# 64-bit weights turned to float32 by a scaled copy of their high words, with low halves on VectorE and a new order of work

## The chip, the cores and the metric

The kernel runs on one core of a Trainium2 chip. A core has TensorE (PE in the rows, PEld its weight loads), VectorE (DVE), ScalarE (ACT), GpSimd (POOL) and SyncE (SP, which here only issues DMAs). The metric is the time of one execution on the device in microseconds, as the median of several runs.

## The reference

Three stages follow each other: a retention layer, a dense layer with `h - tanh(h)`, and an expert layer whose routing is a greedy assignment over all logits.

```python
batch, n_heads, seq, head_dim = (8, 8, 576, 64)
def _attn_ref(q, k, v):
    scores = scale * np.matmul(q, k.transpose(0, 1, 3, 2))
    Dmat = np.where(rel >= 0, gamma[:, None, None] ** rel[None, :, :], 0.0)
    return np.matmul(scores * Dmat[None, :, :, :], v).astype(np.float32)

n_tokens, d_model, d_ff = (4608, 512, 2048)
'w_in': np.random.randn(d_model, d_ff).astype(np.float32) * (1.0 / np.sqrt(d_model))
'w_out': np.random.randn(d_ff, d_model).astype(np.float32) * (1.0 / np.sqrt(d_ff))
def _moe_ref(x, w_in, w_out):
    h = x @ w_in
    g = h - np.tanh(h)
    return (g @ w_out).astype(np.float32)

N, D, E, F = (4608, 512, 8, 1024)
def _moe2_ref(x, w_gate, w1, w2):
    logits = x @ w_gate
    order = np.argsort(-logits.flatten())   # greedy, each expert takes N // E tokens
    ...
    out[mask] = np.maximum(x[mask] @ w1[e], 0.0) @ w2[e]
```

The factor `1.0 / np.sqrt(...)` is a 64-bit scalar, so `w_in` and `w_out` arrive as 64-bit floats. They reach the chip as pairs of 32-bit words, and the kernel makes float32 values of them itself.

## The kernel before, in words

**Stages.** `phase_ab` does the retention layer and the dense layer, `phase_c` the routing and the experts. Tokens go in 12 blocks of 384 (`n`); a block needs four head pairs (`hp`) of the retention layer, so there are 48 pairs `k`. The hidden width of 2048 is cut in 16 pieces `f`. A step `s` is one layer of one block: `h_mm` multiplies the block with one piece of `w_in`, eight instructions on ACT and DVE (`act_in`, `act_do`) make `h - tanh(h)`, `g_high` and `g_low` split it, and `x2_mm` multiplies it with one piece of `w_out`. All products are made of high and low parts, so every operand is first split in two float32r tiles: the high part by a copy on ACT, the low part by a subtraction on POOL or DVE.

**Weights.** There are 32 halves `j`: 16 pieces of `w_in` and 16 of `w_out`, each 128 x 512 values of 64 bits, 512 KB. A half is loaded (`conv_load`, three buffers, `wst` in the rows), then goes through six steps in `work` (six buffers): `bits` (two DVE instructions, L207 and L208, which take the sign, the exponent and the upper bits of the mantissa from the high word), `low` (ACT, L217, the low word as a number), `square` (ACT, L212, the square of the high word), `plus` (POOL, L222, adds the low bits), `guard` (DVE, L226, sets values that would be too small to zero, by the square), `split_hi` (ACT, L231) and `split_lo` (L237: every third half on DVE, the others on POOL, by `CD = 3`). In all of them the words are read and written where they lie, high and low words in turn, so with gaps of one word.

**Pairs.** `attn_load` loads a pair by four DMAs of 192 KB (L261, tiles named after weight tiles in which they lie: `w1h`, `w1l`, `w0h`, `w0l`), `v_scale` scales its values (two ACT instructions, L272), `attn_scores` (L290) and `attn_kv` (L305) are matmuls, `mask` (L317) and `attn_state` run on DVE, `attn2` (L357, L367) on PE and `attn_out` (L387, tile `xf`) on DVE. Four pairs make a block; its values are split (`x_high`, `x_low`) before the first `h_mm`.

**What sets the order.** The first 12 pairs, the 32 halves and the first 34 steps (blocks 0 and 1 and the first two of block 2) are handed as tasks to a list scheduler (`Tasks`) when the program is built. It takes the ready task that can begin first on its engine, and among equals the one with the highest weight in the table `W`; each task has a cost in microseconds, and a task with a `lock` also holds a port that DVE and POOL share in the plan. What it picks is the order of the instructions on every engine, and each engine then works its queue strictly in that order. From step 34 on, the order is written out by hand and the change does not touch it; steps of blocks 2 to 11 load one pair after another in between. The DMAs of qkv and of the weights are all issued on SP in the planned order; four small tables (`qtab`, `vtab`, `amask`, `cint`) are loaded by DMAs on ACT at the very start.

The lines that the steps below use: L157 to L160 (tables), L200 (load of a half), L207 to L237 (its steps), L261 (load of a pair), L272 (`v_scale`), L305 (`attn_kv`), L426 (`h_mm`), L450 to L456 (`act_do`), L470 (`g_low`), L489 (`x2_mm`), L508 (store of a finished block).

Of the kernel before, what the change touches and what calls it, by code (L numbers as in the profile page):

```python
# [36 lines left out]
W = {'a2': 4, 'bits': -3, 'do0': 2, 'do1': -1, 'do2': -4, 'do3': 2, 'end': 2, 'gate': 1, 'gh': -2, 'h': -3, 'hi': -2, 'in0': 2, 'in1': 4, 'in2': -2, 'in3': -2, 'kv': 1, 'lo': -1, 'load': -2, 'low': -1, 'mask': 1, 'out': 2, 'plus': -1, 'raw': 3, 'square': 1, 'state': 2, 'v': -1, 'x2': -3, 'x2h': -4, 'xl': -1, 'xo': 1}  # L37
# [12 lines left out]
CD = 3  # L50
# [90 lines left out]
def phase_ab(tc, ctx, qkv, wio, wgt, wgk, ident, qtab, vtab, amask, cint, x2d, L):  # L141
# [47 lines left out]
    raw = [r.rearrange("p (w t) -> p w t", t=2) for r in raw]  # L189
# [23 lines left out]

    def low(j):

        lw = at(j)[1]
        nc.scalar.activation(lw, lw.bitcast(U32), AF.Copy, scale=2.0 ** -29)  # L217

    def plus(j):

        _, lw, pi, _ = at(j)
        nc.gpsimd.tensor_tensor(pi, pi, lw, op=OP.add)  # L222

    def guard(j):
        H, _, _, p = at(j)
        nc.vector.scalar_tensor_tensor(p, H.bitcast(F32), F64_TINY ** 2, p, op0=OP.is_ge, op1=OP.mult)  # L226

    def split_hi(j):
        io, f = halves[j]
        WH[io][f] = wtile("h", io, f)  # L230
        nc.scalar.activation(WH[io][f].rearrange("p k m -> p (k m)"), at(j)[3], AF.Copy)  # L231

    def split_lo(j):
        io, f = halves[j]
        WL[io][f] = wtile("l", io, f)
        hi, lo = (w[io][f].rearrange("p k m -> p (k m)") for w in (WH, WL))
        (nc.vector if j % CD == 0 else nc.gpsimd).tensor_tensor(lo, at(j)[3], hi.bitcast(F32), op=OP.subtract)  # L237

# [361 lines left out]
    def layer(s):  # L600
# [657 lines left out]
def lay_out(q, k, v, moe_w_in, moe_w_out, moe2_w_gate, moe2_w1, moe2_w2):  # L1258
# [45 lines left out]
```

## Time and profile before

| | |
|---|---|
| median of 3 runs | 1548.69 us (1546.82 to 1548.99) |
| profiled execution, its own time | 1549.22 us |
| its span (first to last instruction) | 1547.4 us |
| mean granted TensorE clock | 0.975 of full speed |
| busy: PE / DVE / ACT / POOL | 1452.7 / 1132.5 / 759.9 / 558.3 us |
| first matmul of the dense layer (L426) | at 42.83 us |
| last of the 12 planned pairs leaves DVE (L387) | at 101.30 us |
| last use of a half on DVE or POOL | at about 208 us |
| blocks 0 and 1 stored (L508) | at 227.1 and 228.97 us |
| blocks 2 and 3 stored | at 314.77 and 394.28 us |

The page gives busy times of each engine, the chain of waits that ended last, and groups of instructions. A stretch of the trace can be asked for apart: then the busy time of each engine in it, its granted clock and its DMA share are given, also for the instructions of one line alone. Since each engine works its queue in order, what matters is which engine is never idle in a stretch, and what the others wait for in it.

### The profile page before, as it was taken

The page shows a single profiled execution, that of the slowest core. Times are in us where ns is not written, and L with a number is a line of the kernel's source. Part 1 is how long each engine was busy: PE and PEld are TensorE (multiplying, and loading weights), DVE is VectorE, ACT ScalarE, POOL GpSimd, SP SyncE. Part 2 cuts the span into 40 slices and gives each one's busy share as a digit, 9 for nine tenths or more (in the row PEclk, how much of TensorE's full clock was granted, in tenths as well). Part 3 has the DMA queues.
Part 4 walks back from the last instruction along what each step waited for, and adds up shares of the span by engine and source line. Part 5 has one row for each costly group of instructions (what it writes and reads, how often), then busy time and mean ns, then how long its engine had stood idle before and what let it go on. Part 6 is the DMA issues. An engine that isn't in the chain of part 4 may idle for free.

```text
span 1547.4 us, 26175 instructions
## 1 busy us (share of the span) xinstructions
PE 1452.7 (94%) x9500; PEld 1273.1 (82%) x9500; DVE 1132.5 (73%) x2741; ACT 759.9 (49%) x1584; POOL 558.3 (36%) x492
## 2 busy tenths in 40 slices
PE   5989899999999999999999999937999999999997
PEld 4777788899898989898989898826788787887996
DVE  7999966878787878787878787867676776765210
ACT  4767775555656555656555656503332323424421
POOL 4546551212222222222222223225535526446541
PEclk7999999999999999999999999968999999999999
DMA  7622231111111111111111100014433423426220
GB/s 255 199 75 82 80 113 68 43 62 42 62 42 62 42 62 42 62 42 62 42 62 42 63 3 21 1 38 130 135 92 110 135 87 113 135 83 191 90 65 31
DMA packets 48610, 122.43 MB, mean 79 GB/s; under 512 B 6624, under 2 KB 13408, under 8 KB 48224
## 3 DMA queue, kind: packets, MB, share of 16 engines
q1 hardware_dynamic: 41184, 99.80, 19.5%
q0 software_dynamic: 6144, 19.93, 4.0%
q8 instruction: 75, 1.23, 0.3%
q10 hardware_dynamic: 1152, 1.02, 0.2%
q14 instruction: 55, 0.45, 0.1%
HBM read 101.85 MB, written 18.87 MB: 78 GB/s over the span
## 4 chain that ended last, share of the span: by engine, by line
PE 73%; DVE 15%; issue 4%; ACT 3%; POOL 2%; DMA 1%; SPq 0%; ACTq 0%; POOLq 0%; DVEq 0%
PE x L489 21%; PE h L426 21%; PE ff L1189 12%; PE ff L1158 10%; PE pb L290 2%; PE pb L357 2%; PE pb L369 1%; DVE work L208 1%; DVE t L456 1%; DVE t L450 1%; PE tp L1112 1%; PE pb L305 1%; DVE t L452 1%; DVE work L207 1%; DVE h L454 1%
## 5 line engine op out<-in xcount | busy, mean ns | idle before, releaser
L470 POOL TENSOR_TENSOR gl<-t,gh 128x384 fp32r<-128x384 f32 x192 | 200.3, 1043 | 644.3 <-ACT gh L467 560.6
L426 PE MATMUL h<-xh,w0h 128*128 128x384 f32 x704 | 239.7, 340 | 7.4 <-DVE t L456 7.3
L426 PE MATMUL h<-xh,w0l 128*128 128x384 f32 x704 | 237.4, 337 | 0.0
L436 ACT ACTIVATE S<-h 128x384 f32<-128x384 f32 x192 | 93.5, 487 | 285.6 <-PE h L426 285.5
L489 PE MATMUL x<-w1h,gh 128*128 128x512 f32 x576 | 230.7, 400 | 0.7 <-ACT gh L467 0.7
L489 PE MATMUL x<-w1l,gh 128*128 128x512 f32 x576 | 226.1, 393 | 0.0
L489 PE MATMUL x<-w1h,gl 128*128 128x512 f32 x576 | 217.1, 395 | 1.5 <-POOL gl L470 1.0
L450 DVE SCALAR_TENSOR_TENSOR t<-t,S 128x384 f32<-128x384 f32 x192 | 114.2, 595 | 119.8 <-ACT t L439 118.8
L530 DVE SCALAR_TENSOR_TENSOR junk<-x2r,wg 128x512 f32<-128x512 f32 x240 | 167.3, 697 | 5.1
L426 PE MATMUL h<-xl,w0h 128*128 128x384 f32 x704 | 152.3, 337 | 0.3 <-DVE xl L413 0.3
L426 PEld LDWEIGHTS h<-xh,w0h 128*128 128x128 f32 x704 | 132.4, 188 | 18.5 <-DVE t L456 11.6
L1075 POOL TENSOR_TENSOR w2l<-ws,w2h 128x512 fp32r<-128x512 f32 x64 | 82.5, 1292 | 161.1 <-ACT w2h L1074 158.9
L426 PEld LDWEIGHTS h<-xh,w0l 128*128 128x128 f32 x704 | 132.7, 189 | 6.9
L489 PEld LDWEIGHTS x<-w1h,gl 128*128 128x128 f32 x576 | 108.1, 188 | 29.9 <-POOL gl L470 5.8
L1189 PE MATMUL ff<-w2h,hh 128*128 128x512 f32 x320 | 127.5, 398 | 3.1 <-DVE hl L1171 2.0
L456 DVE COPY_PREDICATED t<-m,h 128x384 f32<-128x384 uint16 x192 | 114.5, 596 | 21.5 <-ACT m L445 1.7
L1189 PE MATMUL ff<-w2l,hh 128*128 128x512 f32 (+1 forms) x320 | 127.3, 398 | 0.6 <-POOL w2l L1075 0.6
L439 ACT ACTIVATE t<-S,bias 128x384 f32<-128x384 f32 x192 | 118.3, 616 | 17.6 <-POOL gl L470 1.1
L426 PEld LDWEIGHTS h<-xl,w0h 128*128 128x128 f32 x704 | 126.1, 188 | 0.9 <-DVE xl L413 0.9
L489 PEld LDWEIGHTS x<-w1h,gh 128*128 128x128 f32 x576 | 108.1, 188 | 22.8 <-ACT gh L467 1.4
L489 PEld LDWEIGHTS x<-w1l,gh 128*128 128x128 f32 x576 | 108.2, 188 | 17.0
L1158 PE MATMUL ff<-xh,w1h 128*128 128x288 f32 x512 | 115.2, 303 | 6.3 <-DVE hl L1171 5.5
(212 smaller groups left out, 2988.2 us busy)
## 6 DMA issues: line engine op xcount, KB each, us to landing
ws<-in_w SPq DMA_DIRECT2D x128, 256.0 KB, 3.1
ain<-in_qkv SPq DMA_DIRECT2D x36, 768.0 KB, 4.2
wst<-in_wio SPq DMA_DIRECT2D x32, 512.0 KB, 3.6
x2d<-x2r SPq DMA_DIRECT2D x33, 256.0 KB, 2.0
w1h<-in_qkv SPq DMA_DIRECT2D x12, 192.0 KB, 4.0
w1l<-in_qkv SPq DMA_DIRECT2D x12, 192.0 KB, 4.1
w0h<-in_qkv SPq DMA_DIRECT2D x12, 192.0 KB, 3.9
w0l<-in_qkv SPq DMA_DIRECT2D x12, 192.0 KB, 3.8
```

The lines of the kernel that those rows point to most:

```text
L290: nc.tensor.matmul(PSA[k][a][:, chunk(c)], kt[r, chunk(c)], q[r, chunk(c)], start=True, stop=True)
L426: nc.tensor.matmul(h[:, :TB], w[0][f][:, hp, :], x, start=i == 0, stop=i == 11)
L436: nc.scalar.activation(S, h, AF.Square, scale=KSC)
L439: nc.scalar.activation(AT[s][2], AT[s][1], AF.Square, bias=bias[:, 0:1])
L450: nc.vector.scalar_tensor_tensor(t, t, PA - PB * PB / 4, S, op0=OP.add, op1=OP.mult)
L456: nc.vector.copy_predicated(t, m.bitcast(U16), h)
L470: nc.gpsimd.tensor_tensor(G[s][1], TT.pop(s), G[s][0].bitcast(F32), op=OP.subtract)
L489: nc.tensor.matmul(X2[n][i], g[:, i * 128:i * 128 + 128], w, start=(f == 0 and g is gh and w is wh), stop=(f == NF - 1 and g is gl))
L530: nc.vector.scalar_tensor_tensor(j, r, 1.0, wg[e // 4][:, e % 4, :], op0=OP.mult, op1=OP.mult, accum_out=L[:, c, e:e + 1])
L1075: nc.gpsimd.tensor_tensor(l, s, h.bitcast(F32), op=OP.subtract)
L1158: nc.tensor.matmul(ps[u], w[:, k, :], x[:, k, 288 * u:288 * u + 288], start=i == 0, stop=i == 11)
L1189: nc.tensor.matmul(o, h, w, start=f == 0 and i == 0, stop=f == 7 and i == len(prods) - 1, skip_group_check=t == 4)
```

## The change

The two DVE steps `bits` and `guard` and the ACT step `square` become `shrink` (ACT) and a shorter `bits` (DVE). `shrink` reads the high word as a float32 and multiplies it by 2^-112, which moves the exponent to its place and sets too small values to zero; it writes the result without gaps into `work`. `low` now writes its words without gaps too, into the first half of the load buffer. `bits` then shifts by three into the second half of the load buffer (`tensor_scalar`, L216 of the new file) and joins the sign (`scalar_tensor_tensor`, L217), all without gaps. `plus` and `split_hi` stay, and a load buffer is free after `plus`, not after `guard`. `CD` goes from 3 to 1, so every `split_lo` (L233) is on DVE. The tables that ACT loads first change their order (`cint` first, `qtab` last). The weights `W` and the costs of tasks are new, so the list is made anew: the same tasks apart from those above come in another order.

```diff
-CD = 3
+CD = 1
...
-    nc.scalar.dma_start(out=qt, in_=qtab)
+    nc.scalar.dma_start(out=ci[:, :4], in_=cint)
     nc.scalar.dma_start(out=vt[:, :12], in_=vtab)
     nc.scalar.dma_start(out=am, in_=amask)
-    nc.scalar.dma_start(out=ci[:, :4], in_=cint)
+    nc.scalar.dma_start(out=qt, in_=qtab)
...
     def at(j):
-        return raw[j % 3][:, :, 1], raw[j % 3][:, :, 0], work[j % 6], work[j % 6].bitcast(F32)
+        r = raw[j % 3]
+        return r.rearrange("p (w t) -> p w t", t=2), r[:, :DM], r[:, DM:], work[j % 6]
+
+    def shrink(j):
+
+        words, _, _, p = at(j)
+        nc.scalar.activation(p.bitcast(F32), words[:, :, 1].bitcast(F32), AF.Copy, scale=2.0 ** -112)
+
+    def low(j):
+
+        words, lw, _, _ = at(j)
+        nc.scalar.activation(lw, words[:, :, 0].bitcast(U32), AF.Copy, scale=2.0 ** -29)
 
     def bits(j):
-        H, _, pi, _ = at(j)
-        nc.vector.tensor_scalar(pi, H, ci[:, 0:1], ci[:, 1:2], op0=OP.logical_shift_left, op1=OP.bitwise_and)
-        nc.vector.scalar_tensor_tensor(pi, H, ci[:, 2:3], pi, op0=OP.bitwise_and, op1=OP.bitwise_or)
-
-    def square(j):
-        H = at(j)[0].bitcast(F32)
-        nc.scalar.activation(H, H, AF.Square)
...
+        _, _, t, p = at(j)
+        nc.vector.tensor_scalar(t, p, ci[:, 0:1], None, op0=OP.logical_shift_left)
+        nc.vector.scalar_tensor_tensor(p, p, ci[:, 1:2], t, op0=OP.bitwise_and, op1=OP.bitwise_or)
...
-    def guard(j):
-        H, _, _, p = at(j)
-        nc.vector.scalar_tensor_tensor(p, H.bitcast(F32), F64_TINY ** 2, p, op0=OP.is_ge, op1=OP.mult)
...
-        add(("raw", j), SP, DMA_HALF, lambda: conv_load(j), get("guard", j - 3), [get("raw", j - 1)])
-        add(("bits", j), VE, 1.05, lambda: bits(j), get("raw", j), get("lo", j - 6), lock=1.05)
-        add(("low", j), AE, 0.52, lambda: low(j), get("raw", j))
-        add(("square", j), AE, 0.52, lambda: square(j), get("bits", j))
-        add(("plus", j), GE, 1.23, lambda: plus(j), get("bits", j), get("low", j), lock=1.23)
-        add(("guard", j), VE, 0.65, lambda: guard(j), get("square", j), get("plus", j), lock=0.65)
-
+        add(("raw", j), SP, DMA_HALF, lambda: conv_load(j), get("plus", j - 3), [get("raw", j - 1)])
+        add(("shrink", j), AE, 0.58, lambda: shrink(j), get("raw", j), get("lo", j - 6))
+        add(("low", j), AE, 0.58, lambda: low(j), get("shrink", j))
+        add(("bits", j), VE, 1.12, lambda: bits(j), get("low", j), lock=1.12)
+        add(("plus", j), GE, 1.31, lambda: plus(j), get("bits", j), lock=1.31)
```

How the queues stand, at the three places that the prediction speaks of. On ACT, the start of the program before, after the four table loads (`wst_100` and `wst_101` hold the first three halves, `w0h_108` and `w0h_112` the values of pairs 0 and 1):

```order
L217 ACT_TABLE_LOAD
L217 ACTIVATE wst_100<-wst_100 128x512
L212 ACTIVATE wst_100<-wst_100 128x512
L217 ACTIVATE wst_100<-wst_100 128x512
L217 ACTIVATE wst_101<-wst_101 128x512
L212 ACTIVATE wst_100<-wst_100 128x512
L231 ACTIVATE w0h_159<-work 128x512
L212 ACTIVATE wst_101<-wst_101 128x512
L272 ACTIVATE w0h_108<-w0h_108,vt 128x3x64 x2
L272 ACTIVATE w0h_112<-w0h_112,vt 128x3x64 x2
```

Seven steps of the weights stand ahead of the values of pair 0. The same place on ACT now (L268 is `v_scale`, L207 `shrink`, L212 `low`, L227 `split_hi`, L405 `x_high`):

```order
L268 ACT_TABLE_LOAD
L268 ACTIVATE w0h_108<-w0h_108,vt 128x3x64 x2
L268 ACTIVATE w0h_112<-w0h_112,vt 128x3x64 x2
L207 ACTIVATE work<-wst_100 128x512
L212 ACTIVATE wst_100<-wst_100 128x512
L207 ACTIVATE work<-wst_100 128x512
L212 ACTIVATE wst_100<-wst_100 128x512
L227 ACTIVATE w0h_231<-work 128x512
```

The values of pairs 0 and 1 now come first, then two halves. On SP, which issues the loads, the start before:

```order
L200 DMA wst_100<-in_wio 128x1024 x2
L200 DMA wst_101<-in_wio 128x1024
L261 DMA w1h_106<-in_qkv 128x384
L261 DMA w1l_107<-in_qkv 128x384
L261 DMA w0h_108<-in_qkv 128x384
L261 DMA w0l_109<-in_qkv 128x384
```

Three halves are loaded ahead of pair 0. The start on SP now:

```order
L257 DMA w1h_106<-in_qkv 128x384
L257 DMA w1l_107<-in_qkv 128x384
L257 DMA w0h_108<-in_qkv 128x384
L257 DMA w0l_109<-in_qkv 128x384
L257 DMA w1h_110<-in_qkv 128x384
L257 DMA w1l_111<-in_qkv 128x384
L257 DMA w0h_112<-in_qkv 128x384
L257 DMA w0l_113<-in_qkv 128x384
L198 DMA wst_100<-in_wio 128x1024 x2
L257 DMA w1h_114<-in_qkv 128x384
```

Pairs 0 and 1 go first, then two halves, then pair 2. On DVE, in the stretch after the last planned pair, where layers and halves alternate, before:

```order
L207 TENSOR_SCALAR work<-wst_101,ci 128x512
L208 SCALAR_TENSOR_TENSOR work<-wst_101,ci,work 128x512
L207 TENSOR_SCALAR wst_101<-wst_100,ci 128x512
L208 SCALAR_TENSOR_TENSOR wst_101<-wst_100,ci,wst_101 128x512
L450 SCALAR_TENSOR_TENSOR t<-t,S 128x384
L452 TENSOR_TENSOR t<-t,h 128x384
L454 TENSOR_TENSOR h<-T,h 128x384
L456 COPY_PREDICATED t<-m,h 128x384
L450 SCALAR_TENSOR_TENSOR t<-t,S 128x384
L226 SCALAR_TENSOR_TENSOR work<-wst_101,work 128x512
```

Two halves' `bits` stand together ahead of a layer, and a `guard` inside the next. In the same stretch now (L446 to L452 are the four steps of a layer, L233 `split_lo`, L216 and L217 `bits`):

```order
L446 SCALAR_TENSOR_TENSOR t<-t,S 128x384
L448 TENSOR_TENSOR t<-t,h 128x384
L450 TENSOR_TENSOR h<-T,h 128x384
L233 TENSOR_TENSOR w1l_1456<-work,w1h_1450 128x512
L452 COPY_PREDICATED t<-m,h 128x384
L216 TENSOR_SCALAR wst_100<-wst_101,ci 128x512
L217 SCALAR_TENSOR_TENSOR wst_101<-wst_101,ci,wst_100 128x512
L446 SCALAR_TENSOR_TENSOR t<-t,S 128x384
```

Each layer now carries one `split_lo` and one `bits`. Up to the last planned pair there are 13 halves and 7 layers on DVE, where before there were 17 `bits` and 6 layers. After it 19 halves are left, spread over 22 layers up to the last `split_lo`, where before 15 were spread over 22.

## Rows read from the trace of the kernel before

**Rows 1.** The page: busy time of each engine, and the chain by engine.

```profile
PE 1452.7 (94%) x9500; PEld 1273.1 (82%) x9500; DVE 1132.5 (73%) x2741; ACT 759.9 (49%) x1584; POOL 558.3 (36%) x492
PE 73%; DVE 15%; issue 4%; ACT 3%; POOL 2%; DMA 1%; SPq 0%; ACTq 0%; POOLq 0%; DVEq 0%
```

**Rows 2.** Stretches: start:end, length, busy us of each engine, clock, DMA, GB/s.

```profile
core 0: us, PE busy (x) PEld busy (x) DVE busy (x) ACT busy (x) POOL busy (x), PEclk, DMA share, GB/s
0.00:16.23 16.23, 5.72 (x26) 2.42 (x26) 7.17 (x11) 6.05 (x10) 5.19 (x8) 0.85 0.77 261
16.23:42.83 26.60, 20.63 (x212) 15.76 (x212) 24.10 (x48) 16.03 (x33) 14.22 (x11) 0.71 0.78 268
42.83:101.30 58.47, 50.55 (x443) 40.52 (x442) 54.49 (x104) 38.16 (x75) 30.57 (x24) 0.94 0.47 146
101.30:205.70 104.40, 96.34 (x467) 83.12 (x468) 96.94 (x140) 77.72 (x154) 61.77 (x47) 1.00 0.20 66
205.70:229.00 23.30, 22.68 (x114) 20.25 (x114) 15.37 (x28) 18.15 (x39) 9.58 (x9) 1.00 0.35 134
315.00:394.50 79.50, 79.44 (x502) 71.32 (x501) 63.90 (x156) 44.52 (x96) 18.77 (x18) 1.00 0.15 50
```

**Rows 3.** Who waited for whom, PE, 0 to 230 us: total, times, longest.

```profile
PE h L426 <- DVE t L456: 13.0, 16, 3.5
```

**Rows 4.** Timeline of PE: start, length, what, [idle before and releaser].

```profile
9.09 0.94 PE L290 MATMUL ps<-w1h,w1l 64*128 64x128 f32 x12 [3.06 <-DMA w1l<-in_qkv]
16.23 1.25 PE L305 MATMUL ps<-w0h,w0l 128*64 128x64 f32 x12 [6.20 <-ACT w0h L272]
42.83 0.45 PE L426 MATMUL h<-xh,w0h 128*128 128x384 f32 x1
```

**Rows 5.** Timeline of ACT at the start.

```profile
5.09 0.68 ACT L217 ACTIVATE wst<-wst 128x512 int32<-128x512 uint32 x1 [0.76 <-DMA wst<-in_wio]
15.17 0.67 ACT L212 ACTIVATE wst<-wst 128x512 f32<-128x512 f32 x1 [1.59 <-DVE work L208]
15.74 1.48 ACT L272 ACTIVATE w0h<-w0h,vt 128x192 f32<-128x192 f32 x4
```

**Rows 6.** Stretches for L207, L208, L226, L237 in turn: before 16.23, and 0 to 230.

```profile
0.00:16.23 16.23, 2.59 (x3) 0.85 0.77 261
sum 230.00, DVE 25.93; mean DVE 5.19
0.00:16.23 16.23, 3.17 (x3) 0.85 0.77 261
sum 230.00, DVE 36.68; mean DVE 7.34
0.00:16.23 16.23, 0.68 (x1) 0.85 0.77 261
sum 230.00, DVE 26.98; mean DVE 5.40
0.00:16.23 16.23, 0.69 (x1) 0.00 (x0) 0.85 0.77 261
sum 230.00, DVE 9.33 POOL 30.71; mean DVE 1.87 POOL 6.14
```

**Rows 7.** Lines L207 and L208: duration min/median/max in ns.

```profile
L207 DVE TENSOR_SCALAR work<-wst,ci x22: 534/544/1505, 8.8 to 196.7; 128x512 int32<-128x512 int32 x22
L208 DVE SCALAR_TENSOR_TENSOR work<-wst,ci,work x22: 751/754/1701, 9.4 to 197.5; 128x512 int32<-128x512 int32 x22
```

**Rows 8.** Timelines of POOL and DVE, one stretch held by another engine.

```profile
10.30 1.46 POOL L222 TENSOR_TENSOR work<-work,wst 128x512 int32<-128x512 int32 x1 [8.61 <-DVE work L208]
...
10.65 1.67 DVE L208 SCALAR_TENSOR_TENSOR work<-wst,ci,work 128x512 int32<-128x512 int32 x1
```

**Rows 9.** Groups by line, 0 to 230 us: count, busy us, mean ns, idle before.

```profile
L470 POOL TENSOR_TENSOR gl<-t,gh 128x384 fp32r<-128x384 f32 x33 | 37.4, 1133 | 61.3 <-ACT gh L467 41.3 <-issue 9.6 <-PE x L489 5.2
L212 ACT ACTIVATE wst<-wst 128x512 f32<-128x512 f32 x32 | 21.6, 674 | 24.6 <-DVE work L208 15.0 <-DVE wst L208 9.5
```

More of the change, by code (lines that the diff above doesn't have):

```diff
@@ L35 @@
 WARM = 14
-W = {'a2': 4, 'bits': -3, 'do0': 2, 'do1': -1, 'do2': -4, 'do3': 2, 'end': 2, 'gate': 1, 'gh': -2, 'h': -3, 'hi': -2, 'in0': 2, 'in1': 4, 'in2': -2, 'in3': -2, 'kv': 1, 'lo': -1, 'load': -2, 'low': -1, 'mask': 1, 'out': 2, 'plus': -1, 'raw': 3, 'square': 1, 'state': 2, 'v': -1, 'x2': -3, 'x2h': -4, 'xl': -1, 'xo': 1}
+W = {'a1': 3, 'a2': 0, 'bits': -4, 'do0': 0, 'do1': -3, 'do2': -4, 'do3': -2, 'end': -3, 'gate': -1, 'gh': -1, 'gl': 1, 'h': 0, 'hi': 0, 'in0': 1, 'in1': 4, 'in2': -1, 'in3': -3, 'kv': 2, 'lo': -2, 'load': 3, 'low': -2, 'mask': -2, 'out': 2, 'plus': -1, 'raw': 3, 'shrink': -2, 'state': -2, 'v': 2, 'x2': 0, 'x2h': -4, 'xh': 1, 'xl': 1, 'xo': 3}
 SLACK = 0.0
@@ L188, in phase_ab @@
     raw = [wst[0][:, :2 * DM], wst[0][:, 2 * DM:], wst[1][:, :2 * DM]]
-    raw = [r.rearrange("p (w t) -> p w t", t=2) for r in raw]
     work = [bw.tile([128, DM], I32, tag="x2r", name="work", bufs=3) for _ in range(3)]
@@ L199, in conv_load @@
         io, f = halves[j]
-        nc.sync.dma_start(out=raw[j % 3], in_=wio[f, io].bitcast(I32).rearrange("p (w t) -> p w t", t=2))
+        nc.sync.dma_start(out=raw[j % 3], in_=wio[f, io].bitcast(I32))
     def at(j):
-        return raw[j % 3][:, :, 1], raw[j % 3][:, :, 0], work[j % 6], work[j % 6].bitcast(F32)
-    def bits(j):
-        H, _, pi, _ = at(j)
-        nc.vector.tensor_scalar(pi, H, ci[:, 0:1], ci[:, 1:2], op0=OP.logical_shift_left, op1=OP.bitwise_and)
-        nc.vector.scalar_tensor_tensor(pi, H, ci[:, 2:3], pi, op0=OP.bitwise_and, op1=OP.bitwise_or)
-    def square(j):
-        H = at(j)[0].bitcast(F32)
-        nc.scalar.activation(H, H, AF.Square)
-    def low(j):
-        lw = at(j)[1]
-        nc.scalar.activation(lw, lw.bitcast(U32), AF.Copy, scale=2.0 ** -29)
-    def plus(j):
-        _, lw, pi, _ = at(j)
-        nc.gpsimd.tensor_tensor(pi, pi, lw, op=OP.add)
-    def guard(j):
-        H, _, _, p = at(j)
-        nc.vector.scalar_tensor_tensor(p, H.bitcast(F32), F64_TINY ** 2, p, op0=OP.is_ge, op1=OP.mult)
+        r = raw[j % 3]
[6 more added lines that the diff above has]
+        nc.scalar.activation(lw, words[:, :, 0].bitcast(U32), AF.Copy, scale=2.0 ** -29)
+    def bits(j):
+        _, _, t, p = at(j)
+        nc.vector.tensor_scalar(t, p, ci[:, 0:1], None, op0=OP.logical_shift_left)
+        nc.vector.scalar_tensor_tensor(p, p, ci[:, 1:2], t, op0=OP.bitwise_and, op1=OP.bitwise_or)
+    def plus(j):
+        _, lw, _, p = at(j)
+        nc.gpsimd.tensor_tensor(p, p, lw, op=OP.add)
     def split_hi(j):
@@ L230, in split_hi @@
         WH[io][f] = wtile("h", io, f)
-        nc.scalar.activation(WH[io][f].rearrange("p k m -> p (k m)"), at(j)[3], AF.Copy)
+        nc.scalar.activation(WH[io][f].rearrange("p k m -> p (k m)"), at(j)[3].bitcast(F32), AF.Copy)
     def split_lo(j):
@@ L236, in split_lo @@
         hi, lo = (w[io][f].rearrange("p k m -> p (k m)") for w in (WH, WL))
-        (nc.vector if j % CD == 0 else nc.gpsimd).tensor_tensor(lo, at(j)[3], hi.bitcast(F32), op=OP.subtract)
+        (nc.vector if j % CD == 0 else nc.gpsimd).tensor_tensor(lo, at(j)[3].bitcast(F32), hi.bitcast(F32), op=OP.subtract)
     pairs = [(n, hp) for n in range(NB) for hp in range(4)]
@@ L566, in conv_half @@
         io, f = halves[j]
-        add(("raw", j), SP, DMA_HALF, lambda: conv_load(j), get("guard", j - 3), [get("raw", j - 1)])
-        add(("bits", j), VE, 1.05, lambda: bits(j), get("raw", j), get("lo", j - 6), lock=1.05)
-        add(("low", j), AE, 0.52, lambda: low(j), get("raw", j))
-        add(("square", j), AE, 0.52, lambda: square(j), get("bits", j))
-        add(("plus", j), GE, 1.23, lambda: plus(j), get("bits", j), get("low", j), lock=1.23)
-        add(("guard", j), VE, 0.65, lambda: guard(j), get("square", j), get("plus", j), lock=0.65)
+        add(("raw", j), SP, DMA_HALF, lambda: conv_load(j), get("plus", j - 3), [get("raw", j - 1)])
[3 more added lines that the diff above has]
+        add(("plus", j), GE, 1.31, lambda: plus(j), get("bits", j), lock=1.31)
         old = {p: get("a2", 8 + late.index((io, f, p)) // 4) if (io, f, p) in late else None for p in "hl"}
-        add(("hi", j), AE, 0.52, lambda: split_hi(j), get("guard", j), old["h"])
-        us = 0.62 if j % CD == 0 else 1.23
+        add(("hi", j), AE, 0.55, lambda: split_hi(j), get("plus", j), old["h"])
+        us = 0.68 if j % CD == 0 else 1.36
         add(("lo", j), VE if j % CD == 0 else GE, us, lambda: split_lo(j), get("hi", j), old["l"], lock=us)
@@ L614, in layer @@
         add(("gh", s), AE, 0.41, lambda: g_high(s), get("do", s, 3), get("x2", s - 2))
-        add(("gl", s), GE, 0.96, lambda: g_low(s), get("gh", s), lock=0.96)
+        add(("gl", s), GE, 1.04, lambda: g_low(s), get("gh", s), lock=1.04)
         if s == NJ:
@@ L1267, in lay_out @@
     wio = np.ascontiguousarray(np.stack([wi, moe_w_out.reshape(NF, 128, DM)], axis=1)).view(np.int64)
-    cint = np.tile(np.array([3, 0x3FFFFFF8, 0xC0000000, 0xFF800000], np.uint32).view(np.int32), (128, 1))
+    cint = np.tile(np.array([3, 0x80000000, 0, 0], np.uint32).view(np.int32), (128, 1))
     g = np.array(GAM)
```

5 lines of the change are left out of this document (2 added, 3 removed).

## The prediction

> **What bounds the kernel now.** I read the page first, for the engine that fills the span; then the stretches, for where it is not filled; then who PE waits for there, and the rows of the waited-for engine line by line. Over the whole span PE is busy 94% and holds 73% of the chain, DVE 15% [rows 1]. From 315 us on, in a whole block, PE is busy 79.44 of 79.5 us: nothing done to the weights can help there, since their last half is through at about 208 us. The change acts on the first 229 us, up to the store of blocks 0 and 1. There the reader is to see two things [rows 2]. From 16.23 to 205.70 us DVE is busy 24.10 + 54.49 + 96.94 = 175.5 of 189.5 us, 93%, while PE has 167.5 us: DVE is the bound, and PE's idle time in front of the layers is put down to DVE, 13.0 us [rows 3]. Up to 16.23 us nobody is the bound: PE stands 6.20 us for the scaled values of pair 0 [rows 4], which on ACT stand behind a square that waits for DVE [rows 5].
>
> **Part 1, the start.** Before, the first `attn_kv` runs at 16.23 us [rows 4], after the scaling at 15.74 us [rows 5]. Now pair 0 is the first thing SP issues and its scaling the first on ACT. Before, the first 512 KB on SP were there at 5.09 us, when `low` began on them [rows 5]; the three tiles that `attn_kv` needs are 576 KB, so some 5.3 us, plus half of the four scalings (1.48 us [rows 5]), 6.1 us. The scores took 0.94 us [rows 4] and can begin when the warm-up matmuls are through at about 6 us. So `attn_kv` runs at about 7.0 us: **9.2 us** earlier. Against that, the first half now lands behind eight tiles: 1.5 MB and its own 0.5 MB at the 261 GB/s of that stretch [rows 2] are 8 us, with the start some 10 us, and `shrink` and `low` at 0.67 us each [rows 9] end at about 11.3 us. On DVE `bits` of that half stands ahead of the mask of pair 1, and DVE is there at about 9 us: I take **2.5 us** off. Pairs 2 and 3 come earlier too, since three loads of halves no longer stand in front of them. Left are 6.7 us, with 0 and 9.2 as ends: 0 if each later pair's data comes no earlier than before.
>
> **Part 2, the weights on DVE.** Before, the four DVE lines of the weights take 25.93 + 36.68 + 26.98 + 9.33 = 98.9 us, 3.09 a half [rows 6]. Of it 2.59 + 3.17 + 0.68 + 0.69 = 7.1 us lie before 16.23 us, in idle time; 91.8 us lie in the stretch that DVE bounds. Now a half costs three DVE instructions. The nearest rows, undisturbed: the shift as L207, 0.54 us [rows 7]; the joining as L226, which has two tensors too, one of them without gaps, 0.68 us; the low half 0.69 us [rows 6]: 1.9 us. But the lines are stretched: L208 takes 0.75 us alone [rows 7] and 1.67 us beside an addition on POOL [rows 8]. Before, the stretch is 98.9 - 32 x (0.54 + 0.75 + 0.68) - 11 x 0.69 = 28.3 us. I put it down to POOL's 92 two-tensor instructions up to 230 us (33 of L470 [rows 9], 32 additions, 21 low halves, 6 of the split of x). Now 21 of these are gone: 28.3 x 71 / 92 = 21.8 us, 0.68 a half, so 2.6 us. The shift without gaps may be shorter than L207, which no row shows; I take **2.45 us a half**, with 1.9 (no stretch) and 2.8 (each line as stretched as now: 0.81 + 1.15 + 0.85) as ends. All 32 halves now lie in the stretch: 32 x 2.45 = 78.4 us for 91.8, so **13.4 us** less, with ends of 31 and 2.2. No load of DVE moves to POOL: POOL loses 30.71 us of low halves [rows 6].
>
> By the Trainium skill (VectorE: DVE Perf Modes, The perf-mode tier table) a 32-bit `tensor_scalar` from SBUF to SBUF runs at two elements a cycle and an instruction with two tensors at one. Estimated with that page's measured fixed term of about 150 cycles, the shift would take 0.42 us, and the sum would come out 4 us lower (32 x 0.12). L207, with gaps, took 0.54 us [rows 7], and no run here shows the shift without them.
>
> **Part 3, ACT.** Three ACT steps a half before (`low`, `square`, the high part), three now, each with the same 512 elements: costed at nothing. What covers it is ACT's slack, 77.72 of 104.4 us busy from 101.3 to 205.7 us [rows 2]. What goes is the 24.6 us that ACT stood in front of L212 for DVE [rows 9]; what comes is `shrink`, which waits for its load and for the low half of six halves ago. Behind it on ACT stand the squares and bends of the layer, for which DVE waits. A load buffer is free one DVE step earlier than before, and the DMAs are only 20% busy in that stretch [rows 2].
>
> **Part 4, the new order.** Up to the last planned pair 13 halves and 7 layers, before 17 and 6; afterwards one half a layer. The totals stay, so I cost it at nothing by itself, but the stretch is now near PE's own length: PE has 190.2 us of work from 16.23 to 229 us, of 212.8 [rows 2]. For layers that wait out of step although DVE has time I take **2 us** off; the ends are 0 and 8.
>
> **The sum.** 9.2 - 2.5 + 13.4 - 2 = 18.1 us. PE would then be idle about 22.6 - (18.1 - 6.7) = 11 us between the first `attn_kv` and the store of block 1, so there is room for it. Blocks 2 to 11 and the experts are only moved. The profiled execution took 1549.2 us: 1531.1 us. It lies 0.5 us above the median of the runs shown, so 1530.6, rounded to **1530.5 us**.
>
> **The rivals.**
> *PE becomes the bound.* If the three DVE steps come out undisturbed (1.9 us a half), DVE gives back 31 us, more than PE can use. PE's idle time of 22.6 us, the start of 6.7 us and at most 20.63 x 0.29 = 6 us from the clock of 0.71 up to 42.83 us [rows 2] make 35 us; with PE as dense as 98%, about 31: 1518 us. For it: PE fills block 3 wholly. Against: POOL's additions stay.
> *ACT or the loads hold it.* With one half a layer, ACT has about 2.0 us of weights and five steps of the layer in the 4.2 us that PE needs for a layer; a `shrink` that waits then delays the layer's square. If this costs 10 us over 22 layers, 8 remain: 1541 us. Loads that bring the pairs no earlier (end 0 of part 1) give 1537 us. Against: DMA and ACT have the slack named above.
> *Slower: the low halves on DVE wait for POOL.* The sum is 6.7 - 2 + 91.8 - 32 p for a cost of p a half, zero at p = 3.0 us. The longest rows of L207 and L208 are 1.5 and 1.7 us [rows 7]; if two of the three steps waited out an addition as in rows 8, p would be 1.9 + 2 x 0.7 = 3.3: 9 us slower, 1558 us. For it: every half has `bits`, then its addition on POOL, then a low half on DVE, and layers' g_low in between. Against: POOL has 21 instructions fewer to wait for. The Trainium skill (GPSIMD Engine Reference, Specifications) says that the engine shares its SBUF interfaces with VectorE and that instructions with two SBUF inputs contend; by that rule, moving 21 low halves to DVE makes 21 more instructions that can be held. Rows 8 agree with the rule.
> *It doesn't do what it says.* If words without gaps are no faster (joining 0.75, shift 0.54), p is 2.65, the gain 11.7 us: 1537 us, inside the forecast. If in addition the start moves nothing, 1543 us. A result within 0.2%, about what a measurement of this kernel can tell from no change (3 us), needs p of 2.9 to 3.1.
>
> **How the numbers follow.** Forecast (p of 2.2 to 2.7, 1523 to 1539 us): 0.52. PE bound, 1515 to 1522: 0.17. ACT or loads, 1540 to 1545: 0.17. No change: 0.06. Slower: 0.08. The range runs from 1516 to 1544, which leaves out the slower cases, no change and the outermost part of both neighbours, some 0.2. Faster 0.86, same 0.06, slower 0.08.
>
> **What would show it.** Right: first `attn_kv` at about 7 us, first `h_mm` at about 29 us (before 42.83: 6.7 us from part 1, and on DVE three halves ahead of it, 7.4 us, where before four to five stood, some 14 us at 3.09), the last planned pair at about 87 us, blocks 0 and 1 stored at about 211 us, the three DVE lines of the weights together near 78 us, the blocks after that 79.5 us apart. Wrong: first `h_mm` after 36 us (loads), DVE lines of the weights over 97 us (contention), ACT busy over nine tenths with DVE waiting for it (ACT), or a change behind block 2, which no step here gives.

## The result and the profile after

The changed kernel takes 1532.63 us (median of 4 runs, 1530.84 to 1532.82) where the kernel before, beside it, takes 1548.57: a ratio of 0.9897, 95% interval 0.9879 to 0.9914. It is 15.9 us faster; 18.1 were forecast. The profiled execution has a span of 1530.9 us for 1547.4.

The page of the kernel after, busy time and chain, against [rows 1]:

```profile
PE 1450.2 (95%) x9500; PEld 1271.9 (83%) x9500; DVE 1113.3 (73%) x2730; ACT 758.7 (50%) x1584; POOL 525.5 (34%) x471
...
PE 77%; DVE 11%; issue 4%; ACT 3%; POOL 2%; DMA 2%; SPq 0%; POOLq 0%; ACTq 0%; DVEq 0%
```

DVE's share of the chain fell from 15% to 11%, and DVE is 19.2 us less busy. 18.2 of it lie ahead of the stores of blocks 0 and 1, now issued at 210.30 and 212.18 us. The stretches after, as in [rows 2] (length, busy us of each engine, clock, DMA share, GB/s), cut at the first `attn_kv`, the first `h_mm`, the last planned pair and the last low half:

```profile
8.13:28.51 20.38, 15.59 (x189) 11.94 (x189) 15.44 (x38) 12.15 (x26) 5.72 (x5) 0.84 0.91 315
28.51:89.81 61.30, 56.60 (x487) 45.55 (x486) 54.06 (x111) 43.91 (x86) 22.85 (x18) 0.94 0.50 164
89.81:197.00 107.19, 99.22 (x486) 86.62 (x485) 99.62 (x149) 83.50 (x164) 54.85 (x42) 1.00 0.23 80
197.00:212.20 15.20, 15.20 (x78) 13.67 (x77) 10.35 (x20) 13.21 (x29) 5.50 (x6) 1.00 0.53 205
298.00:377.50 79.50, 79.44 (x501) 71.30 (x501) 64.04 (x156) 44.66 (x95) 18.77 (x18) 1.00 0.15 51
```

A whole block takes 79.5 us as before; what comes after the planned part is only moved. In the stretch from 89.81 to 197 us DVE is still busy 99.62 of 107.19 us, 93%, and PE 92.6%. The shares alone do not tell which of the two sets its length; the kernel with the shift done twice, below, does. The same work as one stretch, of the kernel after and then of the kernel before, each up to the store of block 1:

```profile
0.00:212.20 212.20, 192.47 (x1259) 160.27 (x1260) 179.84 (x317) 154.55 (x307) 90.08 (x76) 0.97 0.41 141
```

```profile
0.00:228.97 228.97, 195.88 (x1258) 162.04 (x1259) 198.07 (x328) 156.08 (x307) 121.29 (x97) 0.94 0.39 131
```

This pair is the whole balance. The store moved by 16.8 us. DVE has 18.2 us less work and 11 instructions fewer (96 for 107 of the weights). PE stands 13.4 us less (19.7 for 33.1), and its own work is 3.4 us shorter, for the same number of matmuls (1259 for 1258), with a granted clock of 0.97 for 0.94.

The four lines on DVE that tell the price, as sums of stretches up to 212.2 us (in turn the shift L216, the joining L217, the low half L233, and L446, the first DVE instruction of each layer's bend), against [rows 6]:

```profile
89.81:212.20 122.39, 9.63 (x19) 1.00 0.27 95
sum 212.20, DVE 16.39; mean DVE 5.46
89.81:212.20 122.39, 15.99 (x19) 1.00 0.27 95
sum 212.20, DVE 26.43; mean DVE 8.81
89.81:212.20 122.39, 21.81 (x20) 1.00 0.27 95
sum 212.20, DVE 31.01; mean DVE 10.34
89.81:212.20 122.39, 23.70 (x26) 1.00 0.27 95
sum 212.20, DVE 31.11; mean DVE 10.37
```

The weights take 16.39 + 26.43 + 31.01 = 73.8 us, 2.31 a half, where they took 98.9. But L446 takes 31.11 us for 34 instructions; before it was L450, and took 25.84. Before first, then after (minimum/median/maximum in ns):

```profile
L450 DVE SCALAR_TENSOR_TENSOR t<-t,S x34: 532/550/1672, 47.9 to 225.8; 128x384 f32<-128x384 f32 x34
```

```profile
L446 DVE SCALAR_TENSOR_TENSOR t<-t,S x34: 533/560/1652, 34.8 to 209.0; 128x384 f32<-128x384 f32 x34
L448 DVE TENSOR_TENSOR t<-t,h x34: 537/554/556, 35.4 to 209.7; 128x384 f32<-128x384 f32 x34
...
L216 DVE TENSOR_SCALAR wst<-work,ci x22: 470/476/904, 13.0 to 188.6; 128x512 int32<-128x512 int32 x22
L217 DVE SCALAR_TENSOR_TENSOR work<-work,ci,wst x22: 750/752/1667, 13.5 to 189.1; 128x512 int32<-128x512 int32 x22
L233 DVE TENSOR_TENSOR w0l<-work,w0h x11: 686/859/1782, 17.0 to 185.3; 128x512 fp32r<-128x512 f32 x11
```

The instruction has not changed and its minimum is the same; it is held more often: 16 of the 34 take over 0.6 us, before 8. The counterpart of [rows 8], POOL and then DVE:

```profile
161.17 1.61 POOL L222 TENSOR_TENSOR work<-work,wst 128x512 int32<-128x512 int32 x1
```

```profile
160.92 0.71 DVE L446 SCALAR_TENSOR_TENSOR t<-t,S 128x384 f32<-128x384 f32 x1 [0.59 <-ACT t L435]
161.55 1.78 DVE L233 TENSOR_TENSOR w0l<-work,w0h 128x512 fp32r<-128x512 f32 x1
```

The low half begins 0.38 us into the addition and ends 0.55 us after it. Alone it takes 0.69.

### The profile page after: what moved, and what is told of

Read it like the earlier page. It is cut to its first block, busy times and chain, and to the rows that moved or that the text cites. A ratio compares the mean times of both kernels' runs of the same rounds, so it can differ in the third digit from the quotient of the medians.

```text
span 1530.9 us, 26107 instructions
## 1 busy us (share of the span) xinstructions
PE 1450.2 (95%) x9500; PEld 1271.9 (83%) x9500; DVE 1113.3 (73%) x2730; ACT 758.7 (50%) x1584; POOL 525.5 (34%) x471
## 4 chain that ended last, share of the span: by engine, by line
PE 77%; DVE 11%; issue 4%; ACT 3%; POOL 2%; DMA 2%; SPq 0%; POOLq 0%; ACTq 0%; DVEq 0%
PE h L422 22%; PE x L485 22%; PE ff L1183 12%; PE ff L1152 10%; PE pb L286 2%; PE pb L353 2%; PE pb L365 1%; DVE t L446 1%; PE tp L1106 1%; PE pb L301 1%; DVE t L452 1%; DVE t L448 1%; POOL w2l L1069 1%; DVE work L217 1%; DMA wst<-in_wio 1%
## 5 line engine op out<-in xcount | busy, mean ns | idle before, releaser
L446 DVE SCALAR_TENSOR_TENSOR t<-t,S 128x384 f32<-128x384 f32 x192 | 119.7, 623 | 119.7 <-ACT t L435 118.8
L422 PEld LDWEIGHTS h<-xh,w0h 128*128 128x128 f32 x704 | 132.4, 188 | 13.7 <-DVE t L452 6.4
L452 DVE COPY_PREDICATED t<-m,h 128x384 f32<-128x384 uint16 x192 | 114.5, 596 | 19.6 <-ACT wst L207 0.5
L435 ACT ACTIVATE t<-S,bias 128x384 f32<-128x384 f32 x192 | 118.3, 616 | 18.2 <-POOL gl L466 1.1
L485 PEld LDWEIGHTS x<-w1l,gh 128*128 128x128 f32 x576 | 108.2, 188 | 19.2 <-DVE w1l L233 2.5
```

Source lines behind the costliest of these rows:

```text
L422: nc.tensor.matmul(h[:, :TB], w[0][f][:, hp, :], x, start=i == 0, stop=i == 11)
L435: nc.scalar.activation(AT[s][2], AT[s][1], AF.Square, bias=bias[:, 0:1])
L485: nc.tensor.matmul(X2[n][i], g[:, i * 128:i * 128 + 128], w, start=(f == 0 and g is gh and w is wh), stop=(f == NF - 1 and g is gl))
```

## The experiments

All ratios are to the kernel before on the same chip; differences between ratios are turned into time with 1549 us. I call it **stretch** when a DVE line takes longer than the minimum of its instructions times their number (0.47, 0.75, 0.685 and 0.535 us for shift, joining, low half and L446).

**Order and steps apart.** The first kernel has the new steps with the old table, the second the old steps with the new one.

```diff
-W = {'a1': 3, 'a2': 0, 'bits': -4, 'do0': 0, 'do1': -3, 'do2': -4, 'do3': -2, 'end': -3, 'gate': -1, 'gh': -1, 'gl': 1, 'h': 0, 'hi': 0, 'in0': 1, 'in1': 4, 'in2': -1, 'in3': -3, 'kv': 2, 'lo': -2, 'load': 3, 'low': -2, 'mask': -2, 'out': 2, 'plus': -1, 'raw': 3, 'shrink': -2, 'state': -2, 'v': 2, 'x2': 0, 'x2h': -4, 'xh': 1, 'xl': 1, 'xo': 3}
+W = {'a2': 4, 'bits': -3, 'do0': 2, 'do1': -1, 'do2': -4, 'do3': 2, 'end': 2, 'gate': 1, 'gh': -2, 'h': -3, 'hi': -2, 'in0': 2, 'in1': 4, 'in2': -2, 'in3': -2, 'kv': 1, 'lo': -1, 'load': -2, 'low': -1, 'mask': 1, 'out': 2, 'plus': -1, 'raw': 3, 'square': 1, 'state': 2, 'v': -1, 'x2': -3, 'x2h': -4, 'xl': -1, 'xo': 1}
```

> The new steps of the weights, but the old table W, so the list puts three halves ahead of pair 0 again, on SP and on ACT, as before. My theory, two causes that add up: the start is lost (first attn_kv after 13 us, first h_mm after 36 us), the DVE lines of the weights stay near 74 us; some 8 to 12 us of the 16 us remain, 1537 to 1541 us. Rival A, the new order is all of it: 1547 to 1550 us. Rival B, the new steps are all of it: 1531 to 1534 us.

> The old steps of the weights (bits, square, guard, low halves on POOL two times in three) with the new table W, so pairs 0 and 1 go first on SP and ACT. My theory: the start comes early (attn_kv at about 8 us), but DVE has its 99 us of weights in the stretch that it bounds; 4 to 8 us of the gain remain, 1541 to 1545 us. Rival A, the order is all of it: 1531 to 1534 us. Rival B, the steps are all of it: 1547 to 1550 us.

The first came to 0.9962 (0.995 to 0.9974), 6 us faster than before; the second to 1.0111 (1.0082 to 1.0139), 17 us slower. Expected were gains of both: the first is below the 8 to 12 us that were expected, the second is a plain miss. Only together they give 16 us. With the old table the DVE is no busier than after, 1111.8 us, but the pairs come later (the last planned one at 98.06 us, after at 89.81), and PE waits for their data (total, times, longest):

```profile
PE ps L286 <- DMA w1l<-in_qkv: 4.3, 3, 2.9
```

The first `h_mm` is at 33.96 us there, 28.51 after. With the old steps and the new table the first `h_mm` is early too, at 28.72 us, but the last planned pair comes at 98.80, 2.5 us earlier than before, and the store of block 1 at 245.38, for 228.97 before. The longest wait of PE:

```profile
205.33 0.69 PE L426 MATMUL h<-xh,w0l 128*128 128x384 f32 x1 [12.04 <-POOL w0l L237]
```

with, on POOL, the low half that it waits for:

```profile
202.45 1.61 POOL L222 TENSOR_TENSOR work<-work,wst 128x512 int32<-128x512 int32 x1 [0.69 <-issue]
204.03 1.25 POOL L237 TENSOR_TENSOR w0l<-work,w0h 128x512 fp32r<-128x512 f32 x1
```

Up to the store of block 1, PE stands 43.8 us there for 33.1 before, 10.7 more, and its own work takes 201.6 us for 195.9, at a granted clock of 0.90 for 0.94. The one wait of 12.04 us is more than all of the 10.7; the other 5.7 us are PE's slower work. My reading, argued from this wait: the new order puts each half close ahead of the layer that needs it, which holds when a half passes DVE in 2.3 us and not when it needs `bits`, an addition, a `guard` and a slow low half. With the old steps the early start is thus given back. The 17 us are the price of this one order, fitted to other steps; no run tried an early start with an order fitted to the old steps.

**Words with gaps.** The changed kernel, the words in the load buffer laid out as before:

```diff
-        return r.rearrange("p (w t) -> p w t", t=2), r[:, :DM], r[:, DM:], work[j % 6]
+        r = r.rearrange("p (w t) -> p w t", t=2)
+        return r, r[:, :, 0], r[:, :, 1], work[j % 6]
```

> The changed kernel, but low and the shift write their words back with gaps of one word, where they lay; the order is the same on every engine. My theory: gaps cost DVE less than 0.1 us an instruction (shift 0.47 to 0.54, joining 0.75 as it was with gaps), at most 5 us over 32 halves, of which the bound engine passes on a part: 1533 to 1537 us. Rival, the words without gaps are what made DVE faster: the shift and joining go to 1.5 us together and the time to 1540 us or more.

0.9881 (0.9851 to 0.9911), no loss. The shift and the joining:

```profile
L217 DVE TENSOR_SCALAR wst<-work,ci x22: 469/478/927, 11.4 to 185.5; 128x512 int32<-128x512 int32 x22
L218 DVE SCALAR_TENSOR_TENSOR work<-work,ci,wst x22: 750/752/1675, 11.9 to 186.0; 128x512 int32<-128x512 int32 x22
```

They are as short as without gaps, so gaps at the output of the shift and at one input of the joining cost nothing here. The shift still reads words without gaps in this kernel, which `shrink` writes, while L207 read the high words with gaps. That the shift is shorter than L207 (0.54 us [rows 7]) can come from its input without gaps or from the second operation, which it lost; these two were not tried apart.

**Low halves back on POOL.**

```diff
-CD = 1
+CD = 3
```

> The changed kernel with CD = 3: two low halves of three on POOL again, the list made with the new table. Two causes pull apart. DVE loses 21 instructions of 0.97 us, 20 us, and gets back waits for 21 more POOL instructions, at 0.3 to 0.5 us each 6 to 10 us: by DVE's load alone 1523 to 1529 us. Rival, a low half on POOL takes 1.3 to 1.7 us where DVE takes 0.7 alone, and POOL's queue delays g_low and additions: 1534 us or more.

The list is made anew here, so the order differs too. 0.9899 (0.9883 to 0.9916), the same as after, though DVE is 13.4 us less busy. DVE's busy time and, from its waits up to 215 us, the largest:

```profile
PE 1448.8 (94%) x9499; PEld 1271.9 (83%) x9500; DVE 1099.9 (72%) x2709; ACT 758.4 (49%) x1584; POOL 554.4 (36%) x492
```

```profile
DVE t L446 <- ACT t L435: 22.4, 18, 3.9
```

After, that wait is 6.7 us. What DVE is spared here it waits: the 21 low halves take about 1.36 us each on POOL where DVE takes 0.97 (31.01 / 32), so layers seem to come through later (argued from this wait alone), and DVE stands in front of them. Neither place is better.

**Is DVE still the bound?** Each shift is done twice:

```diff
+        nc.vector.tensor_scalar(t, p, ci[:, 0:1], None, op0=OP.logical_shift_left)
         nc.vector.tensor_scalar(t, p, ci[:, 0:1], None, op0=OP.logical_shift_left)
```

> The changed kernel with the shift of every half done twice, into the same words; the order is otherwise the same. That is 32 more DVE instructions of 0.47 us, 15 us. My theory, DVE still bounds the stretch up to the last half: most of it arrives, 10 to 16 us, 1542 to 1549 us. Rival, PE or the order of the waits is the bound now: under 5 us, 1533 to 1537 us.

```profile
PE 1453.2 (94%) x9500; PEld 1271.4 (82%) x9500; DVE 1134.1 (73%) x2762; ACT 761.7 (49%) x1584; POOL 527.3 (34%) x471
```

0.9993 (0.9979 to 1.0006): 14.9 us longer than after for 20.8 us more on DVE, 15.0 of them the bare shifts (32 x 0.47). By the bare time, work added to DVE is paid nearly in full; of the 20.8 us it is 0.72. So DVE still sets the length of this part.

**What the addition on POOL costs.** Three kernels: without it; with it, but its sum written beside, so that no later step of the half waits for it (the load that takes its buffer next still does); and with an instruction of one input in its place. In all three the weights lack the bits that the low words bring.

```diff
-        nc.gpsimd.tensor_tensor(p, p, lw, op=OP.add)
+        pass
```

> The changed kernel without plus: the addition of the low bits on POOL is left out, so the weights lose the last bits of their mantissa; low still runs. The order is otherwise the same. My theory: what stretches DVE's rows late (low halves 1.1 us where 0.68 would do, the first step of a layer 0.9 where 0.55 would do) is waiting for POOL's additions; without them the DVE lines of the weights fall from 74 to under 66 us, PE's 8 us of idle time between 90 and 197 us mostly go, 1523 to 1528 us. Rival, the stretch has another cause or PE's idle time comes from latencies: 1530 to 1533 us.

```diff
-        nc.gpsimd.tensor_tensor(p, p, lw, op=OP.add)
+        nc.gpsimd.tensor_tensor(lw, p, lw, op=OP.add)
```

> Leaving the addition on POOL out brought 16 us more than the changed kernel; the question is whether the addition costs by standing in the chain of a half (DVE joins, POOL adds, ACT and DVE split) or by holding DVE's two-input instructions while it runs. Here POOL makes the same additions at the same places, but writes the sum beside, into the load buffer, and the splits take the value without it, so nobody waits for the sum (the weights lack the last bits of the mantissa). By the theory of contention the time stays that of the changed kernel, ratio about 0.990 to the kernel before, low halves late in the stretch at 1.1 us and the first instruction of the layer at 0.95 us. By the theory of the chain it falls by most of the 16 us, ratio about 0.981, with the same long DVE instructions. Half of each: 0.985.

```diff
-        nc.gpsimd.tensor_tensor(p, p, lw, op=OP.add)
+        nc.gpsimd.tensor_scalar(p.bitcast(F32), p.bitcast(F32), 1.0, None, op0=OP.mult)
```

> The addition on POOL is replaced by an instruction with one tensor as input that works in place (times one), so that it stands in the chain as before, but reads one tensor from SBUF (the weights lack the last bits of the mantissa, since the low words are not added). If it is the second input that holds DVE, the low halves come down to about 0.8 us late in the stretch and the ratio to about 0.983 (with the instruction itself as long as the addition, 1.3 to 1.4 us). If any POOL instruction on SBUF holds DVE, or if the chain is what costs, the ratio stays at 0.990. If the instruction itself is much shorter, below 0.8 us, the chain is shorter too and this run can't tell the two apart.

| | ratio (95%) | DVE busy | stretch of the four lines |
|---|---|---|---|
| after | 0.9897 (0.9879 to 0.9914) | 1113.3 | 25.8 us |
| no addition | 0.9793 (0.9776 to 0.9809) | 1095.5 | 8.5 us |
| sum written beside | 0.9900 (0.9883 to 0.9916) | 1114.8 | 26.9 us |
| one input | 0.9835 (0.9818 to 0.9851) | 1102.9 | 16.2 us |

The groups of L446 up to 212 us (count, busy us, mean ns), without the addition (where it is L445), with the sum beside, and with one input; of the last also the POOL line:

```profile
L445 DVE SCALAR_TENSOR_TENSOR t<-t,S 128x384 f32<-128x384 f32 x36 | 21.9, 607 | 12.7 <-ACT t L434 12.6
```

```profile
L446 DVE SCALAR_TENSOR_TENSOR t<-t,S 128x384 f32<-128x384 f32 x34 | 31.0, 911 | 8.3 <-ACT t L435 8.2
```

```profile
L446 DVE SCALAR_TENSOR_TENSOR t<-t,S 128x384 f32<-128x384 f32 x36 | 26.6, 739 | 12.7 <-ACT t L435 12.6
...
L222 POOL TENSOR_SCALAR work<-work 128x512 f32<-128x512 f32 x22 | 36.6, 1664 | 26.4 <-DVE work L217 26.4
```

Without the addition the time falls by 16.1 us, about twice what I had expected: I had named the first step of a layer as stretched, but put a number on the weights' lines alone. The second kernel says which half of the addition it is: with all additions still there and no step waiting for them, nothing is won (0.9900). So it is not the place of the addition in the chain of a half; it is that DVE is held while POOL adds: stretch 25.8 us with it, 8.5 without, a difference of 17.3 us for 16.1 us of time. The third confirms it from the other side: POOL's instruction is longer (1.66 us for 1.46), stands in the chain as before, and yet the time falls by 8.4 us with 9.6 us of stretch (0.9835 against 0.9889 of the changed kernel run beside it). A third way in which the addition could cost, by delaying `g_low` in POOL's queue so that PE waits for it, fails: in the lists of the waits of PE, ACT and DVE up to 212 us, of the kernel after, none is put down to `g_low`.

The traces show what the 25.8 us are made of, when the stretch of each DVE instruction is put down to what POOL was running as it began. 16.1 us fall on DVE instructions that began while an addition ran, 9.2 on those that began while a `g_low` ran. Without the addition 5.9 us are left by `g_low`: with it, `g_low` runs later and meets L446 more often (9 times held, without it 4). So the 17.3 us are mostly holds by the addition itself and in a small part holds by a `g_low` that it has pushed back.

By the Trainium skill (Trainium Architecture — The Big Picture, Three mental-model corrections) DVE and GpSimd share a port pair that is locked for one of them and not split. The row at 161.55 agrees for two-input instructions: the low half ends 0.55 us after the addition, and so it does all seven times that it began beside one. L446 ends 0.41 to 0.42 us after the addition, and the same after `g_low`, which reads two tensors of floats, so the type of the words is not what matters. In the kernel with one input the same pair reads, POOL and then DVE:

```profile
112.41 1.79 POOL L222 TENSOR_SCALAR work<-work 128x512 f32<-128x512 f32 x1
```

```profile
112.77 1.09 DVE L233 TENSOR_TENSOR w0l<-work,w0h 128x512 fp32r<-128x512 f32 x1
```

Here the low half ends 0.34 us before the POOL instruction does, and it does so all six times (0.33 to 0.34). It is let go some 0.9 us earlier, counted from the end of POOL's instruction. So the price does not go by the length of POOL's instruction alone. That the second input makes the difference fits all these rows, but the two instructions differ in their operation too, and this was not tried apart.

**The start.** `v_scale` stands first on ACT and waits there for pair 0; the table load (1.28 us) comes behind that wait (ACT of the kernel after):

```profile
6.33 1.28 ACT L268 ACT_TABLE_LOAD   x1 [6.33 <-DMA w0h<-in_qkv]
7.63 0.80 ACT L268 ACTIVATE w0h<-w0h,vt 128x192 f32<-128x192 f32 x2
```

and on DVE the bits of the first half stand ahead of the mask of pair 1, so that PE stands for it:

```profile
13.02 0.49 DVE L216 TENSOR_SCALAR wst<-work,ci 128x512 int32<-128x512 int32 x1 [2.15 <-ACT wst L212]
```

```profile
14.81 2.01 PE L353 MATMUL ps<-ms,w0h 128*64 128x128 f32 x12 [3.17 <-DVE ms L313]
```

The first kernel brings the table load forward with a dummy instruction of one column, the second also moves the first bits and their addition behind that mask.

```diff
+    nc.scalar.activation(bias[:, 2:3], bias[:, 0:1], AF.Copy)
```

```diff
+            (lambda: held.append(lambda: bits(j))) if j == 0 else lambda: bits(j)
...
+            (lambda: held.append(lambda: plus(j))) if j == 0 else lambda: plus(j)
...
+            (lambda: (mask(), [f() for f in held])) if k == 1 else mask
```

> The changed kernel with one ACTIVATE of one column on ACT ahead of the scaling of pair 0, so the load of ACT's function table (1.28 us), which now stands behind the wait for pair 0's values and ends at 7.6 us, is done while they are on their way. The order is otherwise the same. My theory, the start is on the path: attn_kv at about 7.0 us instead of 8.1, 0.5 to 1.3 us less, 1531 to 1532 us. Rival: DVE waits for the first half until 13 us anyway, nothing changes, 1532 to 1533 us.

> As the run with the early table, and bits and plus of the first half stand behind the mask of pair 1 on DVE and POOL instead of ahead of it. Now DVE waits from 10.9 to 13.0 us for that half while the mask of pair 1 is ready, and PE stands 3.2 us for the mask. My theory, part 1's hold of 2.5 us is this: first h_mm 2 to 4 us earlier, 1528 to 1530.5 us. Rival, the load of DVE up to the last half sets the end and the idle time is only moved: 1531 to 1533 us.

> The changed kernel itself once more, on the same chip and against the same runs as its neighbours, so that differences of 1 to 3 us can be read: ratio 0.988 to 0.991, blocks 0 and 1 stored at 210 and 212 us.

> The version with the table load early and the bits and the addition of the first half behind the mask of pair 1, beside the changed kernel on the same chip. By its trace it stored blocks 0 and 1 2.8 us earlier; if that is real the time is 2 to 3 us lower than that of the changed kernel run beside it (ratio about 0.002 lower). If not, both are within 1 us.

The early table load alone: 0.9894 (0.9877 to 0.991), no difference to the changed kernel that the intervals show. Its first `attn_kv` is at 7.52 us and not at 8.13, but in the second trace of the changed kernel it is at 7.70, so 0.4 of these 0.6 us already lie between two executions of one kernel. Both edits: 0.9882 (0.9866 to 0.9899), and in the second comparison 0.9872 (0.9855 to 0.9888), 1530.11 us, beside the changed kernel's 0.9889 (0.9872 to 0.9905), 1532.39 us. The runs of the two hardly overlap (1528.37 to 1530.94 and 1530.63 to 1532.97), so 2 us is likely real, but the intervals of the ratios do overlap. Between these two traces the first `h_mm` is 0.8 us earlier (26.80 for 27.62), not 2 to 4 as expected, and the store of block 0 1.0 us (208.02 for 209.00). By its median it is the fastest version that computes all of the reference.

## Why the prediction was right

**The start** came nearly as foretold at each of its marks; what it is worth in time was not measured by itself. First `attn_kv` at 8.13 us, foretold 7; PE stands 1.03 us there for the scaled values, which the table load holds back (before, it stood ahead of a step of the weights; now it waits with `v_scale`). The prediction had taken it as done, but with the load brought forward `attn_kv` still came at 7.52. First `h_mm` at 28.51, foretold 29. The last planned pair came at 89.81, foretold 87; blocks 0 and 1 stored at 210.3 and 212.2, foretold 211. The hold for the first half was foretold as 2.5 us; PE's wait for that mask is 3.17 us, in the second trace 2.70, and the version that takes it away, with the table early, is about 2 us faster, not clear of the noise.

**The weights on DVE** were foretold at p = 2.45 us, 78.4 us, and came at 73.8, p = 2.31. The bare times were 0.47 + 0.75 + 0.69 = 1.91 us, foretold 1.9, but by two errors that cancel: the shift was shorter (0.47 for 0.54), the joining longer (0.75 for 0.68), as L208 did (0.75) and not L226. The estimate from the perf-mode table of the Trainium skill (VectorE: DVE Perf Modes), 0.42 us for the shift, was nearer than L207 and still below the measured 0.47.

**The step that was wrong** is the stretch: 0.68 a half was taken from POOL's 92 and 71 instructions and put on the weights' lines alone. There it is only 0.40 a half (12.9 us, where the lines of before had 28.3), while L446, which no step of the prediction names, went from a stretch of 7.6 us to 12.9. With it the sum of the term is 91.8 - 73.8 - 5.3 = 12.7 us for the 13.4 foretold. Counted over these five lines before and four after, stretch went from 35.9 to 25.8 us, 0.72 of it, for 71 / 92 = 0.77 of the instructions: for this pair the rule came out, its address did not. It does not carry to other pairs: without the additions 39 of the 71 instructions are left, 0.55, but 0.33 of the stretch.

**ACT at nothing** holds: busy 83.50 of 107.19 us, 78%, and DVE waits 6.7 us for L435 where it waited 8.1 for L439.

**The order** was costed at nothing with 2 us off. For the pair as built more was lost: of 12.7 us on DVE less 3.2 for the hold, 9.5 us, only 5.1 came through to PE (next paragraph), so 4.4 for the 2, inside its ends of 0 and 8. The term also hides the finding of the first two experiments: steps and order are worth -6 and +17 us apart and -16 together. The prediction could not have summed them one by one.

**PE's idle time** was foretold as 11 us between the first `attn_kv` and the store of block 1; it is 204.07 - 186.61 = 17.5. The prediction's own terms give 13.7, as the hold of 2.5 us is idle time too. What the time lost there came back from a place that the sum leaves out: PE's work in this part is 186.6 us for 190.2, at a higher granted clock from the first `attn_kv` to the first `h_mm` (0.84 after, 0.71 before); PE was idle there for 4.8 of 20.4 us after, 6.0 of 26.6 before. The prediction had that gain in a rival only, at up to 6 us. By PE, then, the store of block 1 moved by 8.1 us of earlier start, 5.1 us less of idle time (22.6 - 17.5) and 3.6 us of shorter work, 16.8 in all. The prediction had 9.2, 8.9 (13.4 - 2.5 - 2) and nothing. That the total is near although 3.8 of the 8.9 us did not come, since 3.6 came from a place outside the sum, is luck.

Of the **rivals**, PE as the bound fails (DVE at 93% in the longest stretch, and added work costs nearly its full bare price), ACT and the loads fail by the rows above. The price of the first was good all the same: without the addition a half takes 66.8 / 32 = 2.09 us on DVE, and 0.9793 of 1549.2 is 1517 us, where that rival has 1518. "Slower" needed p over 3.0; p was 2.31. "It doesn't do what it says" holds in part: gaps at the places tried cost nothing, and the joining came at its 0.75, but the shift at 0.47 and not 0.54.

## What to carry to other kernels

When work moves between two engines of which one holds the other, sum the stretch over every line on the held engine, not over the lines that change: here the weights' lines were spared 15.4 us of it and L446 took 5.3 back. An instruction on POOL that costs POOL nothing, being idle time there, can cost DVE half a microsecond each (17.3 us for 32 additions, the `g_low` that they push back included), so the first question to a DVE-bound stretch is what POOL runs beside it, and with how many inputs. And a list of work fitted to one set of steps is part of those steps: of the 16 us the steps alone gave 6, and the list alone cost 17.

## What the hardware showed that I had not expected

- POOL's `tensor_scalar` with one input of 128x512 took 1.61 to 1.66 us as means of its two groups, longer than its addition of two (1.42 to 1.46), and held DVE less (16.2 us of stretch for 25.8): a low half beside it ended 0.33 to 0.34 us before it, beside the addition 0.55 us after it.
- DVE's shift, which reads one tensor, is held as well: 0.47 us alone, up to 0.90; when 21 low halves stand on POOL its mean is 0.63 us (20.2 / 32). It was held to the end by the one-input instruction too: it ended 0.28 to 0.29 us after either.
- DVE instructions with an operand in PSUM were not held: L448, 34 times, 0.537 to 0.556 us, of which 17 ran beside an addition, a `g_low` or a low half of x on POOL.
- Gaps of one 32-bit word at the output of the shift and at one input of the joining cost nothing: 0.47 and 0.75 us with and without.
